# The first batch of a fused attention and MLP kernel: k cast by its transfer, masks added by TensorE, ranks for the first batch, and a first layer in two token ranges

## The chip, the cores and the metric

The kernel runs on one core of one Trainium2 chip. The metric is the device time in microseconds (us) of one execution, the lower the better; the median of several executions is quoted with its range. The figures of one profile are a little shorter than the time of its own execution, because the profile's span starts at the core's first instruction: the profiled execution of the kernel before took 351.13 us and has a span of 349.4.

Engine names: PE is TensorE (PEld its weight loads), DVE is VectorE, ACT is ScalarE, POOL is GpSimd, SP is SyncE.

## The reference, cut to what matters

```python
# q, k, v: (batch 8, heads 8, tokens 576, head size 64), float32
scores = 1/8 * q @ k^T
mask   = (0 <= i - j < 64)                    # causal, window of 64
attn   = softmax(where(mask, scores, -1e9))
x      = (attn @ v) -> (8 * 576 tokens, 512)
h      = x @ w_in                             # 512 x 2048
out    = (h * sigmoid(h)) @ w_out             # 2048 x 512, float32
```

## The kernel before

The program is written by a list scheduler, `Plan`. Every piece of work is added with a class, its cost on each engine that may do it, what it waits for, and a rank. `Plan.run()` plays the costs forward once, when the kernel is built, and always gives a free engine the ready piece with the lowest rank. What reaches the chip is a fixed order of instructions on each engine. So a rank or a cost in this table changes the order and nothing else; on the chip each engine waits for real.

```python
p = Plan(
    {name: len(b) for name, b in banks.items()},
    rank=dict(one=-9, dma=-1, ld0=-1, ld1=-1, st=-2, silu=-3, out=-2, pv=0, ot=0, s=1, moe=99, turn=2,
              norm=0, inverse=0, bridge=0, exp=1, mask=1, lift=2, shift=2, cast=4, late=5),
)
```

Attention is done in units of one head pair and 192 tokens, twelve to a batch. A batch starts by loading q and k, casting them to bf16 (`cast`), transposing them on PE (`turn`) and copying the result out of PSUM (`lift`); v is loaded with a cast and half of it is copied to the other 64 partitions (`shift`). A unit is then this chain:

```python
s  = p.add("s", {"PE": 0.17}, ...)                       # 3 matmuls: scores of keys against queries
ex = p.add("exp", {"ACT": 0.5}, ..., table="exp")
ma = p.add("mask", {"DVE": 0.37}, ..., [ex, c_mask[0]])  # exp times 0 or 1
pv = p.add("pv", {"PE": 0.17}, ...)                      # values, with a column of ones for the sum
rc = p.add("inverse", {"DVE": 0.21}, ...)
no = [p.add("norm", {"DVE": 0.37, "ACT": 0.8}, ...) for hh in range(2)]   # ACT only in batch 0
ot = p.add("ot", {"PE": 0.1}, ...)                       # matmul that transposes back
br = p.add("bridge", {"ACT": 0.34, "DVE": 0.36}, ...)    # to x, transposed, in SBUF
```

The MLP works on tiles of 512 tokens: 64 matmuls of the first layer, 16 silus on ACT, 64 matmuls of the second layer. The exponential and the silu are in different tables of ACT, and `Plan` reckons 1.28 us for each change (the trace has a table load of 1.28 us at 37.33). Tile 0 waits for the bridges of all twelve units of batch 0, since 512 tokens end in its third group:

```python
have = o_done[:NP * ((TB * (j + 1) + 2) // 3)]
...
op = p.add("moe", {"PE": 0.2165}, None, have + [win[ft // 2]], ...)
si = p.add("silu", {"ACT": 0.6}, ..., table="silu")
```

Batch 0's q comes through SP's queue, its k through ACT's, v and the weights through GpSimd's, cast to bf16 on the way. DVE clears the buffer of batch 1's transposed q (`clear_qk(1)`) at the start.

The softmax here doesn't subtract the row's maximum and nothing guards it: scores larger than these inputs give would overflow.

## Time and profile before

| what | figure | where from |
|---|---|---|
| time | 350.98 us (349.42 to 350.98, 3 runs) | timed runs |
| span of the profile | 349.4 us | the page |
| PE busy in the span | 321.9 us, 92% | the page, part 1 |
| first matmul of the MLP | 37.17 us | timeline |
| second layer of tile 0 starts | 60.10 us | timeline |
| first layer of tile 1 starts | 79.85 us | timeline |
| mean granted clock of PE | 0.995 | the run's record |

The prediction shows the stages. Two more views of the page matter later: the clock and the transfers in 40 equal slices of 8.7 us (in tenths), and the chain of work that ended last, by line.

```profile
PEclk9999999899999999999999999999999999999999
DMA  8999999696825967291963900010020011011011
...
PE mp L313 35%; PE mp L322 34%; PE at L284 5%; PE at L235 4%; PE at L270 4%; PE at L304 3%; DMA vv<-in_v_dram 2%; DVE ob L296 1%; DVE qbd L242 1%; ACT qbd L242 1%; ACT ob L300 1%; DVE e L279 1%; ACT g L319 1%; ACT e L276 1%; DVE qbd L184 1%
```

The clock row shows full almost throughout, though up to about 41 us the matmuls went at half pace all the same; the section on the result comes back to this. The transfers are near their fill for most of the first 60 us and busy on and off until about 200 us; after that they have room. The chain is PE's two MLP layers (L313 and L322, 69%) and PE's attention; everything else is a few per cent in all (DVE 6%, ACT 4%, transfers 2%), most of it at the start.

### The profile page before, as it was taken

Reading aid. Unit: us, or ns where it says so; the run is one execution under the profiler, and the core shown is the slowest. Engines: PE = TensorE matmul, PEld = TensorE weight load, DVE = VectorE, ACT = ScalarE, POOL = GpSimd, SP = SyncE. Lnnn points to the kernel's source line nnn. Section 1 sums busy time; section 2 is a strip of 40 time slices with the busy share of each in tenths; the row PEclk is TensorE's granted clock in tenths of the full one; section 3 lists DMA queues with packets and bytes.
Section 4 is the critical chain, followed back from the end, with each engine's and each line's share of the span. In section 5 each row is a group of like instructions: output and inputs, shape, how many; then the busy total and the mean of one; then the engine's idle time right before and its main releaser. Section 6 shows DMA issues by size and latency. Waiting matters only on the chain.

```text
span 349.4 us, 6381 instructions
## 1 busy us (share of the span) xinstructions
PE 321.9 (92%) x2356; PEld 177.5 (51%) x2400; DVE 198.2 (57%) x548; ACT 230.2 (66%) x450; POOL 52.3 (15%) x65
## 2 busy tenths in 40 slices
PE   1566897999999999999999999999999999999995
PEld 1444454655565555665556556655444444444442
DVE  7877395777958987888988896898200000000000
ACT  3667588438889888798968888766617525614611
POOL 8636650040000300211302200000000000000000
PEclk9999999899999999999999999999999999999999
DMA  8999999696825967291963900010020011011011
GB/s 213 188 214 288 188 236 251 57 59 183 243 76 168 188 199 218 70 106 49 137 202 74 85 2 30 34 60 2 0 92 30 0 62 60 0 63 60 0 56 66
DMA packets 61279, 37.64 MB, mean 108 GB/s; under 512 B 39232, under 2 KB 56128, under 8 KB 61248
## 3 DMA queue, kind: packets, MB, share of 16 engines
q0 software_dynamic: 44416, 11.28, 34.8%
q1 hardware_dynamic: 16000, 24.78, 22.7%
q10 hardware_dynamic: 832, 1.18, 1.3%
q8 instruction: 19, 0.31, 0.4%
q14 instruction: 12, 0.10, 0.1%
HBM read 36.70 MB, written 9.44 MB: 132 GB/s over the span
## 4 chain that ended last, share of the span: by engine, by line
PE 85%; DVE 6%; ACT 4%; DMA 2%; issue 2%; POOL 0%; ACTq 0%; DVEq 0%
PE mp L313 35%; PE mp L322 34%; PE at L284 5%; PE at L235 4%; PE at L270 4%; PE at L304 3%; DMA vv<-in_v_dram 2%; DVE ob L296 1%; DVE qbd L242 1%; ACT qbd L242 1%; ACT ob L300 1%; DVE e L279 1%; ACT g L319 1%; ACT e L276 1%; DVE qbd L184 1%
## 5 line engine op out<-in xcount | busy, mean ns | idle before, releaser
L322 PE MATMUL mp<-w_out_sb,g 128*128 128x512 bf16 x550 | 144.2, 381 | 0.9
L313 PE MATMUL mp<-bridge,w_in_sb 128*128 128x512 bf16 x558 | 134.9, 384 | 0.9 <-DMA vv<-in_v_dram 0.2
L319 ACT ACTIVATE g<-mp 128x512 bf16<-128x512 f32 x144 | 83.3, 597 | 22.6 <-PE mp L313 21.8
L313 PEld LDWEIGHTS <-w_in_sb 128*128 128x128 bf16 x576 | 53.5, 99 | 54.5 <-issue 3.0
L322 PEld LDWEIGHTS <-g 128*128 128x128 bf16 x576 | 52.8, 98 | 41.6 <-issue 0.3
L296 DVE TENSOR_TENSOR ob<-at,rc 64x192 bf16<-64x192 f32 x182 | 63.8, 351 | 4.8 <-ACT ob L300 1.3
L205 POOL DMA_DIRECT2D vv<-in_v_dram x32 | 33.0, 1034 | 128.3 <-PE at L284 109.1
L276 ACT ACTIVATE e<-at 128x384 bf16<-128x384 f32 x96 | 42.7, 497 | 9.2 <-PE at L270 8.7
L328 ACT COPY ot<-mp 128x512 f32<-128x512 f32 x23 | 13.4, 585 | 46.4 <-PE mp L322 45.0
L279 DVE TENSOR_TENSOR e<-e,mask 128x384 bf16<-128x384 bf16 x96 | 31.0, 349 | 18.3 <-ACT e L276 17.2
L284 PE MATMUL at<-vv,e 128*128 128x130 bf16 x288 | 32.7, 232 | 3.1 <-DVE ob L296 1.3
L270 PE MATMUL at<-qbd,kt 128*128 128x128 bf16 x288 | 29.6, 231 | 6.2 <-ACT qbd L242 2.6
L235 PE MATMUL at<-ident,natb 96*128 96x96 bf16 x384 | 27.0, 216 | 8.0 <-ACT natb L224 7.1
L284 PEld LDWEIGHTS <-e 128*128 128x128 bf16 x288 | 23.8, 102 | 18.6 <-DVE e L279 2.7
L309 ACT CAST bridge<-at 128x192 bf16<-128x192 f32 x62 | 19.6, 318 | 18.3 <-PE at L304 16.6
L235 PEld LDWEIGHTS <-natb 96*128 96x128 bf16 x384 | 22.6, 103 | 16.6 <-ACT natb L224 8.5
L270 PEld LDWEIGHTS <-kt 128*128 128x128 bf16 x288 | 22.2, 103 | 15.6 <-DVE kt L248 3.6
L304 PEld LDWEIGHTS <-ob 128*128 128x128 bf16 x288 | 19.6, 100 | 20.6 <-DVE ob L296 10.8
L304 PE MATMUL at<-twoi,ob 128*128 128x64 bf16 x288 | 25.5, 199 | 4.5 <-DVE ob L296 2.8
L242 DVE COPY qbd<-at 64x576 bf16<-64x576 bf16 x30 | 22.6, 752 | 9.8 <-PE at L235 8.1
L242 ACT COPY qbd<-at 64x576 bf16<-64x576 bf16 x34 | 21.5, 632 | 7.3 <-DVE qbd L242 6.4
L224 ACT CAST natb<-nat 96x768 bf16<-96x768 f32 x31 | 25.5, 828 | 0.8 <-DMA nat<-in_q_dram 0.8
(35 smaller groups left out, 144.0 us busy)
## 6 DMA issues: line engine op xcount, KB each, us to landing
out_dram<-ot SPq DMA_DIRECT2D x36, 256.0 KB, 2.0
nat<-in_q_dram SPq DMA_DIRECT2D x28, 288.0 KB, 4.5
nat<-in_k_dram SPq DMA_DIRECT2D x24, 288.0 KB, 4.9
vv<-in_v_dram POOLq DMA_DIRECT2D x32, 144.0 KB, 5.8
w_in_sb<-in_moe_w_in_dram POOLq DMA_DIRECT2D x8, 256.0 KB, 10.3
w_out_sb<-in_moe_w_out_dram POOLq DMA_DIRECT2D x8, 256.0 KB, 9.3
nat<-in_k_dram ACTq DMA_DIRECT2D x4, 288.0 KB, 7.2
nat<-in_q_dram POOLq DMA_DIRECT2D x4, 288.0 KB, 10.7
```

The lines of the kernel that those rows point to most:

```text
L205: queue[e].dma_start(out=vv[b % NK][:, 2 * g0 + 1:2 * g1 + 1:2, 0:D], in_=v[b].rearrange("h s d -> (h s) d").rearrange("(g p) d -> p g d", ...
L235: nc.tensor.matmul(pst[:, m], lhsT=natbs[w][:, m], rhs=ident[0:NR, 0:NR], is_transpose=True, start=(m == 0), stop=(m == NM - 1),)
L242: copies[e](out=qbd[b % NK][r, pj, hh].rearrange("x (p m) -> x p m", m=NM), in_=at_bf16(op)[r].rearrange("x (m p) -> x p m", m=NM),)
L270: nc.tensor.matmul(at_sp(op)[:, x], lhsT=kt[b % NK][:, pj * S + t * 64:pj * S + t * 64 + 128], rhs=qbd[b % NK][:, pj, :, t * 64:t * 64 + 6 ...
L276: nc.scalar.activation(out=es[n % NE], in_=at_sp(op), func=ACTF.Exp, scale=scale)
L279: nc.vector.tensor_mul(es[n % NE], es[n % NE], mask0 if g == 0 else mask)
L284: nc.tensor.matmul(at_pv(op)[:, x], lhsT=es[n % NE][:, x].rearrange("p h i -> p (h i)"), rhs=vv[b % NK][:, s:s + NB + 1:NB, 0:D + 1], star ...
L296: nc.vector.tensor_mul(ob[r, :, r], pv[r, :, hh, 0:D], rc[r, :, hh:hh + 1].to_broadcast([64, 3, 64]))
L304: nc.tensor.matmul(banks["at"][op["bank"]][:, 64 * x:64 * x + 64], lhsT=obs[n % NOB][:, x], rhs=twoi, start=(x == 0), stop=(x == 2))
L313: nc.tensor.matmul(banks["mp"][bank["bank"]], lhsT=w_in_sb[:, c, ft * 128:(ft + 1) * 128], rhs=bridge[c][:, j * TT:(j + 1) * TT], start=(c ...
L319: nc.scalar.activation(out=gts[gt], in_=banks["mp"][bank["bank"]], func=ACTF.Silu)
L322: nc.tensor.matmul(banks["mp"][bank["bank"]], lhsT=gts[gt][:, m * 128:(m + 1) * 128], rhs=w_out_sb[:, f, :], start=(f == 0), stop=(f == NF ...
```

## The change

Its intent is to start the MLP earlier. Batch 0 is the only batch that no matmul of the MLP hides, so every microsecond taken out of its chain should move the whole of the rest forward. Six things change for batch 0, for tile 0 and for the clearing. Besides, batch 2's q and k go to GpSimd's queue, `Plan` reckons transfers differently, and its rule for when scores may run among the MLP's matmuls is fitted to the two passes:

1. k is loaded by GpSimd with a cast, in two halves a head pair, straight into the bf16 buffer.
2. The mask is a bias of 0 or -30000, added to the scores by one more matmul; the multiplication on DVE goes.
3. Casts, lifts, shifts and exponentials rank above normalisations.
4. Units go group by group instead of pair by pair.
5. The clearing for batch 1 goes to GpSimd, behind w_in.
6. Tile 0's first layer is done for 384 tokens, which need eight units only, and then for the other 128.

```diff
+        rank0=dict(cast=-6, lift=-5, shift=-4.5, exp=-4, mask=-4, inverse=-3.5, norm=-3, bridge=-3.2),
...
+        for m, a in ((mask, bias), (mask0, bias0)):
+            nc.vector.tensor_scalar(a, m, 1.0, 30000.0, op0=ALU.subtract, op1=ALU.mult)
...
+    def load_k_cast(w, b, pj, hh):
+        nc.gpsimd.dma_start(
+            out=natbs[w][:, :, 64 * hh:64 * hh + 64],
+            in_=k[b, 2 * pj + hh].rearrange("(p m) d -> p m d", m=NM),
...
+    def scores_idle(op, b, pj, g):
+        nc.tensor.matmul(
+            banks["at"][op["bank"]][:, 0:384], lhsT=ident,
+            rhs=(bias0 if g == 0 else bias).rearrange("k x h i -> k (x h i)"), start=True, stop=False)
...  (the three score matmuls follow, with start=False)
-        for g, pj in ([(g, pj) for pj in range(NP) for g in range(NG)] if b == 0 else
-                      [(g, pj) for g in range(NG) for pj in range(NP)]):
+        for g, pj in [(g, pj) for g in range(NG) for pj in range(NP)]:
...
+        parts = [(0, 384), (384, TT)] if j == 0 else [(0, TT)]
+        for lo, hi in parts:
+            have = o_done[:NP * ((j * TT + hi + 191) // 192)]
...
-    c_qk.append(p.add("late", {"DVE": 1.8}, lambda _: clear_qk(1)))
+    c_q[1] = [p.add("dma", {"POOL": 1.3}, lambda e, hh=hh: clear_q(e, 1, hh)) for hh in range(2)]
...
-        lv = [p.add("dma", {"POOL": 1.0}, lambda e, part=part: load_v(e, b, part), busy, dma=2.6)
+        lv = [p.add("dma", {"POOL": 1.0}, lambda e, part=part: load_v(e, b, part), busy, dma=1.25)
```

## The prediction

> **What bounds the kernel now.** I cut the span into stages at places that the timeline names: the first matmul of the MLP (37.17), the end of its slow start (41.9), the end of tile 0's first layer (56.85), the start of its second layer (60.1) and of tile 1's first layer (79.85). The stage table gives each stage's start:end and length, then busy us (and instructions) of PE, PEld, DVE, ACT, POOL, then clock and DMA.
>
> ```profile
> 0.00:37.17 37.17, 18.05 (x156) 13.49 (x158) 28.66 (x84) 22.26 (x58) 23.83 (x36) 1.00 1.44 222
> 37.17:41.90 4.73, 4.73 (x16) 1.97 (x16) 0.00 (x0) 2.62 (x4) 3.41 (x6) 1.00 2.67 176
> 41.90:56.85 14.95, 14.84 (x114) 7.94 (x115) 12.56 (x22) 12.40 (x22) 5.07 (x5) 1.00 1.21 251
> 56.85:60.10 3.25, 1.29 (x12) 0.83 (x12) 1.39 (x6) 3.24 (x7) 0.00 (x0) 0.93 1.49 234
> 60.10:79.85 19.75, 19.56 (x157) 11.15 (x158) 14.70 (x49) 7.74 (x22) 4.00 (x4) 0.93 0.87 65
> 79.85:343.70 263.85, 261.56 (x1900) 141.48 (x1938) 140.92 (x389) 181.32 (x341) 15.98 (x16) 1.00 0.38 84
> ```
>
> From 60.1 on PE is 99% busy: that part is matmul work, which the change hardly touches. All that can be won lies before 60.1, where PE stands for 19.1 us before the MLP and for 2.0 us at 56.85. Before 37.17 the work is batch 0's attention, twelve units (four head pairs by three groups of 192 tokens), and it is paced by DVE (28.66 us busy) and ACT (22.26 us) handing work to each other. The timeline of the first us (start, duration, engine, line, what, and in brackets the idle time and its releaser) shows where that starts badly:
>
> ```profile
> 6.17 1.02 DVE L183 MEMSET qbd<- 64x1152 f32 x1 [0.18 <-issue]
> ...
> 7.47 1.02 DVE L184 MEMSET qbd<- 64x1152 f32 x1 [0.28 <-issue]
> 8.52 0.75 DVE L242 COPY qbd<-at 64x576 bf16<-64x576 bf16 x1
> ...
> 9.30 0.63 ACT L242 COPY qbd<-at 64x576 bf16<-64x576 bf16 x1 [2.67 <-DVE qbd L242]
> ```
>
> DVE clears batch 1's buffer while batch 0's first transposed q waits. At the other end the MLP starts:
>
> ```profile
> 36.32 0.64 PE L304 MATMUL at<-twoi,ob 128*128 128x64 bf16 x3 [0.44 <-ACT ob L300]
> ...
> 37.17 4.47 PE L313 MATMUL mp<-bridge,w_in_sb 128*128 128x512 bf16 x10 [0.22 <-DMA vv<-in_v_dram]
> 37.17 0.15 PEld L313 LDWEIGHTS <-w_in_sb 128*128 128x128 bf16 x1 [0.28 <-issue]
> 37.33 1.28 ACT L319 ACT_TABLE_LOAD   x1
> ```
>
> The chain of waits puts 7.90 us of a v transfer ahead of this matmul. I do not believe it: the matmul reads no v, and PE was idle for 0.22 us only. What it came after is the last unit's normalisation on ACT and its transpose on PE. So the start of the MLP is set by batch 0's last unit.
>
> **What the Trainium skill says.** (1) "TensorE: Matmul & The Clock Gate", "What's actually happening": a PE that has been idle runs at half clock until it has been busy for about 3.4 us. The trace agrees: the first weight loads of L313 come every 0.43 us, later 44 matmuls in a row take 9.66 us, 0.22 each. (2) "ScalarE: Activation LUTs", "What ACT_TABLE_LOAD costs": 1283 ns for the load, about 1380 more for a drain. The trace has 1.28 at 37.33; the silu after it starts at 38.70, so the drain does not show. (3) "DMA: Bandwidth & Descriptors", "SWDGE vs HWDGE vs iDMA": a cast in a transfer can only be issued from GpSimd. The change obeys it: k moves from ACT's queue to GpSimd's. (4) The same page, "Specifications": runs under 512 B do not reach full rate. The k cast writes runs of 64 bf16 elements, 128 B, as v does already; the four v transfers, issued from 1.5 to 4.5, land about 11.2 us later each, but among q, k and w_in, so no row here isolates that cost.
>
> **The change part by part**, with the order of instructions of the changed kernel at hand.
>
> *Clearing.* Batch 1's qbd goes to GpSimd behind w_in. DVE loses 2 x 1.02 plus gaps, 2.3 us, right on the path.
>
> *k by cast transfer.* Four casts of batch 0 vanish (0.83 on ACT or about 0.55 on DVE; the order shows two on each before), the fourth q's cast moves from DVE to ACT, and ACT no longer issues transfers until 3.0. GpSimd issues eight half transfers, then v, then w_in. The last pair's k reuses a buffer that waits for the first k's turn on PE, about 7 us, so v is issued some 7 us later (8.5 to 12.5 instead of 1.5 to 5.6). But v landed only at 12.7 to 15.5 before. With q and k mostly landed I expect 12.5 to 16, no loss. GpSimd keeps eight transfers outstanding (the fifth w_in issue, at 13.04, waited for the first v). So w_in still lands from about 17 to 28 (before: 16.5 to 27), q and k of batch 1 at 28 to 37, w_out at 43 to 54: the same stream, which already runs nearly full, DMA 9 tenths. It must stay ahead of an earlier MLP. Pass A (below) uses a w_in slice every 1.3 us from 27; w_out is wanted from about 51, one slice per 1.73 us. Both hold.
>
> *Masks as a bias.* Twelve multiplications of 0.35 leave DVE, 4.2 us, and a link of ACT to DVE to PE leaves each unit. Two bias tiles cost DVE some 0.6. PE gains twelve 384-column matmuls, 0.165 warm or 0.32 cold, 2 to 4 us in a stage where it was half idle.
>
> *Order.* Units run group by group instead of pair by pair, lifts first, and nine exponentials before most normalisations.
>
> *When the MLP can start.* It needs bridges of eight units. ACT's queue up to the eighth: four casts 3.3, four lifts 2.5, eleven exponentials 5.5, eight normalisations 8 x 0.71 = 5.7, three bridges 1.0: 18.0, from the first q at about 4.7: 22.7 with no waiting. DVE: free at 6.0, then eight lifts 6.0, masks 0.95, v shifts 8 x 0.32 = 2.6, ten reciprocals 2.0, ten normalisations 3.6, five bridges 1.6: 16.7, also 22.7. Two engines feeding each other do not run without gaps; DVE was 77% busy before. At 82 to 85% over the stage I get **27 instead of 37.17**, a gain of 10.2.
>
> *Tile 0 in two passes.* Pass A (384 tokens): 64 matmuls at 0.165, 10.5; six turn groups among them at 0.42, 2.5; a cold start about 1: 14, so 27 to 41. Then a new wait. ACT's queue holds, after the last silu (0.6): table load 1.28, three exponentials 1.5, a normalisation 0.71, another exponential 0.5, the last bridge 0.32: 4.9 until pass B may start, 45.9. PE has only some 2 us of scores and turns for that. Pass B is 64 x 0.055 = 3.5 of PE, but ACT goes first through a lift 0.63 and a table load 1.28, then sixteen silus of about 0.29 (estimate from 0.60 at 512 and 0.83 ns per element): about 5.5 for the stage. **The second layer starts at 51.4 instead of 60.1.** The split therefore returns some 1.5 of the 10.2: two more table loads and PE gaps of about 5.5 in all, against 2.0 before.
>
> *Sum.* 60.1 - 51.4 = 8.7. What follows is the same work for a busy PE. 351.0 - 8.7 = 342.3, rounded to **342**.
>
> **The rivals.** *(a) The transfers bound the start.* If the 128-byte runs make k and v slow in one queue, v lands after 18, values wait, the MLP starts at 30 or later: 345 to 348. For it: v now leaves after k, and DMA has no slack. Against it: bytes are the same, and 15.5 was the last v landing with everything competing. *(b) The two passes give the gain back.* If normalisations of the late units or batch 1's lifts queue ahead of the last bridge, the gap before pass B grows from 3 to 6 or more and PE turns cold again: 345 or more. For it: ACT runs in order and changes tables twice more. Against: batch 0's units are ranked first, and ACT was idle for part of 37 to 57. *(c) ACT and DVE run gapless and PE is warm when the MLP starts*, being denser: start at 25, no slow start: 339. *(d) Hidden anyway*: PE was never the bound before 37 and is after, so an earlier start cannot be swallowed unless w_out binds. It was complete at about 54 and in the new plan is not wanted whole before about 64.
>
> **Range and chances.** The start is uncertain by about 2.5 us each way, the gap and pass B by 2, the rest by 1: together about 3.5. Range 337.5 to 347. Faster by 2% means below 344.0, 2 us above my figure: 0.72. Within 2%: 0.27. Slower needs a stall of 16 us against the plan: 0.01.
>
> **What would show it.** Right: first L343 matmul at 25 to 29; no DVE clearing between 6 and the first lift; v shifts from about 13 without long waits; no mask multiplications before it; a PE gap of 2 to 4 us between passes with ACT's table load in it; second layer at 49 to 54; from there to the end 289.3, as before (349.4 - 60.1), within 1.5. Wrong: PE waiting for v, k or w_in (then a); a second layer that starts late although the first started early (then b); or a longer stretch after the second layer's start, if w_out or batch 1's attention now lags behind PE, which would mean that the gain of the start was only moved.

## More of the kernel before

Every timed run that is compared here was in the fast state. One run (`clear_first`) was a single look, whose state is unknown, and its time is not used.

## The result, and the profile after

The changed kernel took a median of 346.10 us (345.76 to 347.68), against 350.77 (349.42 to 350.98) of the kernel before in the same rounds: a ratio of 0.988, with a 95% interval of 0.985 to 0.992. A ratio here is the mean time of one kernel's fast runs over the mean of the other's fast runs of the same rounds, so it is not quite the ratio of the medians. The same kernel was timed twice more, in later sets (chips 12 and 3): 0.9944 (0.9908 to 0.998; 346.91 us) and 0.9906 (0.9875 to 0.9936; 346.03 us). So the gain is about 0.6 to 1.2%, two to four microseconds. The prediction had 2.5% and a range that ended at 347; the time fell inside the range and the gain is about a quarter to a half of what was forecast.

The first ratio may flatter the change a little. In the later sets every run of the kernel before at 350.1 us or more has a mean clock of 0.995, and every faster one has 1.000. Three of the four runs here have times of the slower group, and so has the profile shown above. The profile of the changed kernel is that of its slowest run (347.68; the others took 345.76 to 346.18).

The stage table of the changed kernel, cut at the same places and with one cut more for the second pass (columns as in the prediction: start:end, length, busy us and instructions of PE, PEld, DVE, ACT, POOL, clock, DMA share, GB/s):

```profile
0.00:30.99 30.99, 17.32 (x156) 12.61 (x157) 22.88 (x65) 17.87 (x47) 24.06 (x38) 0.90 1.30 158
30.99:45.38 14.39, 14.36 (x108) 8.68 (x106) 7.53 (x14) 11.22 (x22) 11.88 (x14) 0.86 1.78 216
45.38:50.81 5.43, 3.35 (x38) 2.31 (x36) 4.83 (x12) 4.42 (x10) 2.45 (x5) 0.81 1.21 227
50.81:57.82 7.01, 6.69 (x87) 6.58 (x86) 5.62 (x18) 5.80 (x19) 2.80 (x5) 0.66 1.13 262
57.82:77.81 19.99, 19.86 (x193) 12.00 (x191) 16.08 (x49) 17.17 (x33) 8.02 (x8) 1.00 1.86 205
77.81:346.00 268.19, 263.77 (x1906) 139.35 (x1905) 136.12 (x384) 171.95 (x329) 16.33 (x16) 1.00 0.37 82
```

The rows are: batch 0, pass A (384 tokens), the gap, pass B (128 tokens), the second layer of tile 0, and the rest. The MLP starts 6.2 us earlier than before (30.99 for 37.17). By the second layer 2.3 us of that is left (57.82 for 60.10). From there to the end it takes 288.2 us, 1.1 less than before (289.3), which with the 2.3 makes the 3.4 by which the span is shorter. The 1.1 need not be the change's: the profile before has 3.2 us at a clock of 0.50 there (59.8 to 63.0), and `before_clear`, without it, takes 288.3. DVE's and ACT's loads in the first row fell as reckoned (28.66 to 22.88, and 22.26 to 17.87), and POOL's is nearly the same.

The same two rows of slices, and the chain by line:

```profile
PEclk9995987999999999999999999999999999999999
DMA  9999999998796656979304800110020011011012
...
PE mp L352 36%; PE mp L343 35%; PE at L314 4%; PE at L253 4%; PE at L288 4%; PE at L334 3%; DMA natb<-in_k_dram 2%; DVE qbd L260 2%; ACT qbd L260 1%; ACT ob L330 1%; DVE vv L274 1%; DVE ob L326 1%; DVE kt L266 1%; DVE vv L276 1%; PE at L300
```

Two things are new in these views. In three slices between 26 and 61 us PE's clock is 0.5 to 0.8, where the row before showed full. That row has to be checked against the pace of the matmuls. In the kernel before, the first ten matmuls of the MLP took 4.47 us (shown in the prediction; their weight loads are 0.43 us apart), twice the 0.22 of later ones, and three score matmuls in a row took 0.52 us at 29.20 against 0.33 at 58.67: half pace, at a shown clock of 1.00. In the changed kernel the pace changes from half (0.53 at 17.37) to full (0.33 at 18.00), again at a shown 1.00. So in these profiles the row tells nothing before its first recorded change, both kernels start at half pace, and both enter the MLP at half pace. And the transfer on the chain is no longer v but `natb<-in_k_dram`, the cast transfer of k. The timeline shows the start of that:

```profile
9.06 1.12 PE L253 MATMUL at<-ident,natb 96*128 96x96 bf16 x12 [3.70 <-DMA natb<-in_k_dram]
...
30.99 1.47 PE L343 MATMUL mp<-bridge,w_in_sb 128*128 128x384 bf16 x4
```

PE turns the first q at 4.70, then waits 3.70 us for the first k. Its two half transfers, issued at 1.56 and 2.3, took 6.9 and 6.7 us to land; the plain transfer of the first k before took 4.5 us from 0.7. And the gap between the passes, as ACT sees it (start, us, engine, line, what, count):

```profile
45.93 1.28 ACT L306 ACT_TABLE_LOAD   x1
47.22 1.25 ACT L306 ACTIVATE e<-at 128x384 bf16<-128x384 f32 x3
48.62 0.71 ACT L330 ACTIVATE ob<-at,rc 64x64 bf16<-64x64 f32 x3
49.23 0.47 ACT L306 ACTIVATE e<-at 128x384 bf16<-128x384 f32 x1
50.16 0.32 ACT L339 CAST bridge<-at 128x192 bf16<-128x192 f32 x1 [0.46 <-PE at L334]
50.93 0.63 ACT L260 COPY qbd<-at 64x576 bf16<-64x576 bf16 x1 [0.45 <-DVE qbd L260]
51.58 1.28 ACT L349 ACT_TABLE_LOAD   x1
```

This is the list that the prediction gave, in the same order: back to the exponential's table, three exponentials, a normalisation, one more exponential, the last bridge; then a lift and the silu's table. The gap is 5.4 us for a predicted 4.9.

### The profile page after: what moved, and what is told of

Same layout as the page of the kernel before. It is cut to its first block, busy times and chain, and to the rows that moved or that the text cites. A ratio compares the mean times of both kernels' runs of the same rounds, so it can differ in the third digit from the quotient of the medians.

```text
span 346.0 us, 6606 instructions
## 1 busy us (share of the span) xinstructions
PE 325.4 (94%) x2476; PEld 181.5 (52%) x2476; DVE 193.1 (56%) x539; ACT 228.4 (66%) x457; POOL 65.5 (19%) x83
## 4 chain that ended last, share of the span: by engine, by line
PE 87%; DVE 6%; ACT 3%; DMA 2%; issue 1%; POOL 0%; DVEq 0%; POOLq 0%; ACTq 0%
PE mp L352 36%; PE mp L343 35%; PE at L314 4%; PE at L253 4%; PE at L288 4%; PE at L334 3%; DMA natb<-in_k_dram 2%; DVE qbd L260 2%; ACT qbd L260 1%; ACT ob L330 1%; DVE vv L274 1%; DVE ob L326 1%; DVE kt L266 1%; DVE vv L276 1%; PE at L300 1%
## 5 line engine op out<-in xcount | busy, mean ns | idle before, releaser
L352 PE MATMUL mp<-w_out_sb,g 128*128 128x512 bf16 x576 | 148.4, 379 | 0.0
L343 PE MATMUL mp<-bridge,w_in_sb 128*128 128x512 bf16 (+2 forms) x640 | 140.7, 367 | 0.5 <-ACT g L349 0.3
L349 ACT ACTIVATE g<-mp 128x512 bf16<-128x512 f32 (+2 forms) x160 | 86.0, 554 | 23.6 <-PE mp L343 21.6
L343 PEld LDWEIGHTS <-w_in_sb 128*128 128x128 bf16 x640 | 59.2, 102 | 51.3 <-issue 1.9
L358 ACT COPY ot<-mp 128x512 f32<-128x512 f32 x29 | 16.9, 586 | 53.8 <-PE mp L352 49.2
L309 DVE TENSOR_TENSOR e<-e,mask 128x384 bf16<-128x384 bf16 x84 | 27.0, 347 | 6.8 <-ACT e L306 6.0
L288 PE MATMUL at<-qbd,kt 128*128 128x128 bf16 x252 | 25.5, 219 | 0.9 <-DVE kt L266 0.5
L320 DVE RECIPROCAL rc<-at 128x6 f32<-128x6 f32 x96 | 18.2, 193 | 12.5 <-PE at L314 10.2
L260 DVE COPY qbd<-at 64x576 bf16<-64x576 bf16 x27 | 20.2, 748 | 8.5 <-ACT qbd L260 6.3
L288 PEld LDWEIGHTS <-kt 128*128 128x128 bf16 x252 | 18.3, 97 | 9.1 <-issue 1.1
```

The lines of the kernel that those rows point to most:

```text
L260: copies[e](out=qbd[b % NK][r, pj, hh].rearrange("x (p m) -> x p m", m=NM), in_=at_bf16(op)[r].rearrange("x (m p) -> x p m", m=NM),)
L288: nc.tensor.matmul(at_sp(op)[:, x], lhsT=kt[b % NK][:, pj * S + t * 64:pj * S + t * 64 + 128], rhs=qbd[b % NK][:, pj, :, t * 64:t * 64 + 6 ...
L309: nc.vector.tensor_mul(es[n % NE], es[n % NE], mask0 if g == 0 else mask)
L343: nc.tensor.matmul(banks["mp"][bank["bank"]][:, lo:hi], lhsT=w_in_sb[:, c, ft * 128:(ft + 1) * 128], rhs=bridge[c][:, j * TT + lo:j * TT + ...
L349: nc.scalar.activation(out=gts[gt][:, lo:hi], in_=banks["mp"][bank["bank"]][:, lo:hi], func=ACTF.Silu)
L352: nc.tensor.matmul(banks["mp"][bank["bank"]], lhsT=gts[gt][:, m * 128:(m + 1) * 128], rhs=w_out_sb[:, f, :], start=(f == 0), stop=(f == NF ...
```

## The experiments

All of them change the changed kernel, unless a text says otherwise. This table has the places of each profile in us and the time; the sets were timed on three chips (sets 1, 2 and 4 on chip 12, set 3 on 14, set 5 on 3), each beside the kernel before, so ratios compare across sets and medians only within one. "Second" is the start of tile 0's second layer, "tile 1" that of tile 1's first layer.

| kernel | MLP | second | tile 1 | median (range) | ratio (95%) |
|---|---|---|---|---|---|
| changed, first profile | 30.99 | 57.82 | 77.81 | 346.10 (345.76 to 347.68) | 0.988 (0.985, 0.992) |
| set 1: k_first_plain | 27.47 | 55.64 | 75.51 | 348.12 (347.08 to 349.64) | 0.996 (0.992, 1.001) |
| k_all_plain | 30.20 | 56.01 | 75.75 | 346.25 (345.12 to 346.87) | 0.990 (0.986, 0.994) |
| clear_dve | 29.03 | 56.16 | 75.54 | 346.38 (345.79 to 346.99) | 0.992 (0.987, 0.996) |
| one_pass | 34.94 | 53.23 | 74.62 | 345.84 (345.36 to 346.66) | 0.990 (0.986, 0.994) |
| set 2: after_again | 30.45 | 57.08 | 77.07 | 346.91 (346.02 to 349.62) | 0.994 (0.991, 0.998) |
| warm | 30.52 | 55.48 | 75.41 | 345.51 (345.27 to 345.93) | 0.990 (0.986, 0.994) |
| mask_mul | 30.91 | 59.75 | 79.82 | 349.89 (349.20 to 350.97) | 1.003 (0.999, 1.006) |
| no_ranks | 31.46 | 58.32 | 78.31 | 348.67 (348.19 to 349.60) | 0.999 (0.996, 1.003) |
| set 3: exp_first | 31.40 | 50.09 | 70.05 | 346.04 (344.26 to 348.18) | 0.988 (0.982, 0.994) |
| exp_first_warm | 32.80 | 51.06 | 70.96 | 348.16 (344.59 to 349.35) | 0.992 (0.986, 0.998) |
| one_pass_warm | 34.90 | 53.40 | 74.73 | 345.59 (344.13 to 345.92) | 0.985 (0.981, 0.990) |
| before_clear | 37.30 | 58.08 | 77.01 | 348.72 (348.17 to 350.61) | 0.996 (0.992, 1.000) |
| set 4: exp_first_lessv | 32.37 | 52.27 | 72.22 | 343.28 (342.35 to 343.51) | 0.981 (0.976, 0.986) |
| after_lessv | 29.85 | 56.73 | 76.73 | 346.60 (345.56 to 346.65) | 0.991 (0.986, 0.995) |
| exp_first_v26 | 32.33 | 55.57 | 75.46 | 345.52 (345.30 to 346.09) | 0.988 (0.984, 0.992) |
| set 5: best | 32.70 | 54.72 | 75.15 | 345.28 (342.56 to 345.64) | 0.986 (0.983, 0.990) |
| after_third | 30.17 | 55.56 | 75.55 | 346.03 (345.24 to 347.11) | 0.991 (0.988, 0.994) |

The theory was that the first k lands late and holds up batch 0's whole chain. Its rivals were that DVE is slowed by what GpSimd does beside it, that PE's half clock costs the time, and that the early start is real but is taken back later by something that the kernel then runs into.

### k back to the plain transfer: the first one, or all

```diff
-                if b == 0 and kk:
+                if b == 0 and kk and not (pj == 0):       # k_first_plain; k_all_plain: never
...
+                    (else) cls, us = ("ld1", {"ACT": 0.45})   # k through ACT's queue, then a cast
```

> The changed kernel, but the first pair's k of batch 0 is loaded as before (ACT's queue, then a cast); the other three pairs keep the cast in the transfer. Theory K (the first k lands at 9.0 instead of about 5.3, PE stands 3.7 us for it, and that delay carries through to the MLP): first k lands near 5.3, first scores near 8 instead of 10.5, first matmul of the MLP near 28.5 instead of 31.0, total 2 us less than the changed kernel (344). Rival P (DVE and GpSimd stand in each other's way at 15 to 24 us, v shifts 0.7 to 1.1 us instead of 0.32, and that backlog sets the start whatever k does): start of the MLP moves by less than 1 us, total within 1 us.

> The changed kernel with all four k of batch 0 loaded and cast as before: only the cast transfer undone. v and w_in are then issued some 7 us earlier. Theory K: first k near 5.3, MLP starts near 28.5 or a little later because four casts (0.55 to 0.83 us) return to DVE and ACT; total 1 to 2.5 us less than the changed kernel. Rival P: the casts return 2 to 3 us of work to the two engines that set the start, so the MLP starts at 31 to 33 and the total is 0 to 2 us more.

With the first k alone by the plain transfer, PE turns it at 7.04, where the three profiles of the changed kernel have 9.06, 8.51 and 8.24:

```profile
7.04 1.14 PE L253 MATMUL at<-ident,natb 96*128 96x96 bf16 x12 [0.45 <-DVE natb L242]
...
27.47 1.16 PE L343 MATMUL mp<-bridge,w_in_sb 128*128 128x384 bf16 x3
```

The MLP starts at 27.47, where the prediction had put it. In the three profiles of the changed kernel the start follows the first k at a fixed distance: 30.99 - 9.06 = 21.93, 30.45 - 8.51 = 21.94, 30.17 - 8.24 = 21.93 (and in `after_lessv`, below, 29.85 - 7.91 = 21.94). So the late k does delay the start. Here the distance is shorter too, 20.43. DVE's eight copies of v were all over before GpSimd's clearing began and took 3.3 us, where the changed kernel's first profile has 4.9; the next experiment is about that. The miss of 4.0 us is thus made of k's landing, 1.2 to 2.0 us, and of a longer way from there.

But the time did not improve: 348.12, with a ratio that is no better than the changed kernel's in any of its three sets. Pass A took 14.9 us, the gap 6.4, pass B 6.8, and from tile 1 to the end it took 269.8 us, against 268.2 in the changed kernel. An earlier start of the MLP is not an earlier end.

With all four k's by plain transfers the first k is turned at 7.07 as well, but the start is 30.2: four casts are back on ACT and DVE, and the distance is 23.1. The time is the changed kernel's. So the cast transfer of k gives with one hand what it takes with the other, and nothing measurable in time comes of it.

### Clearing by DVE instead of GpSimd

```diff
-    c_q[1] = [p.add("dma", {"POOL": 1.3}, lambda e, hh=hh: clear_q(e, 1, hh)) for hh in range(2)]
+    c_q[1] = [p.add("clear", {"DVE": 1.05}, lambda e, hh=hh: clear_q(e, 1, hh)) for hh in range(2)]
```

> The changed kernel with batch 1's qbd cleared by DVE when it is free, not by GpSimd behind w_in. Theory P: the v shift that took 1.11 us while GpSimd cleared (21.45 to 23.65) falls to 0.7 or below, MLP starts 0.5 to 1 us earlier, total 0 to 1 us less. Theory K: start unchanged within 0.5 us, total the same.

> clear_dve once more, one look, beside the runs above on one chip: the MLP's start at 29.0 in its first profile against 30.5 to 31.0 in two profiles of the changed kernel. If GpSimd's clearing costs the start 1.5 us, it comes again at 28.5 to 29.5; if it was chance, 30 to 31.

(`clear_first` is the same file again, for a second profile.) The ground for it was in the changed kernel's timeline. First DVE's copies of v to the other partitions, then what GpSimd did at that time:

```profile
18.64 0.71 DVE L274 COPY vv<-vv 64x576 bf16<-64x576 bf16 x1
...
22.22 0.47 DVE L276 COPY vv<-vv 64x576 bf16<-64x576 bf16 x1
22.72 1.11 DVE L274 COPY vv<-vv 64x576 bf16<-64x576 bf16 x1
```

```profile
15.41 6.00 POOL L229 DMA_DIRECT2D w_in_sb<-in_moe_w_in_dram  x8
21.45 2.20 POOL L194 MEMSET qbd<- 64x1152 f32 x2
```

The same copy, which takes 0.32 us at its shortest, takes up to 0.71 us beside the issues and up to 1.11 beside the memsets. The eight together took 4.9 us where the prediction had 8 x 0.32 = 2.6. With the clearing on DVE, later, the last two copies read:

```profile
20.87 0.32 DVE L276 COPY vv<-vv 64x576 bf16<-64x576 bf16 x1
21.22 0.41 DVE L274 COPY vv<-vv 64x576 bf16<-64x576 bf16 x1
```

and in `clear_first` 0.32 and 0.32. The MLP's start came 20.72 and 20.63 us after the first k instead of 21.93, so 1.2 us earlier; 0.7 of that are the copies (4.2 us in all), and the rest came with the order, which changes a little. This fits the lock that the Trainium skill describes in "SBUF — State Buffer", section "Who interferes with whom": a copy on DVE can take the port pair that it shares with GpSimd, and whichever is second blocks fully. The trace agrees for the memsets. Whether the issues do the same is open: here most copies beside the w_in issues remain at 0.71, but in `k_first_plain` all eight lay beside them (13.76 to 19.89) and took 0.31 to 0.65. In time the experiment is a tie (346.38).

### Tile 0's first layer in one pass

```diff
-        parts = [(0, 384), (384, TT)] if j == 0 else [(0, TT)]
+        parts = [(0, TT)]
```

> The changed kernel with tile 0's first layer in one pass of 512 tokens. Theory S (the split gives back what the early start wins: two more table loads, a 5.4 us gap and a half-clock stretch at 48 to 55): MLP starts near 34, first layer ends near 51, second layer starts near 54.5 instead of 57.8, total 1.5 to 3 us less than the changed kernel. Rival (the split is worth its cost, since PE does 10 us of first layer while the last units finish): second layer starts at 58.5 or later, total 1 us or more above the changed kernel.

The MLP starts 4 us later (34.94), needs no second pass, and reaches the second layer at 53.23, 2.3 to 4.6 us before the three profiles of the changed kernel. Its time, 345.84, is at least as good. So the split buys an early start and pays it back in full: the gap and pass B are 12.4 us in the changed kernel, and 0.5 us here. From the second layer to the end it takes 290.6 us, 2.4 more than in the changed kernel's first profile, so a part of its own lead is lost later too.

### The changed kernel again, with a warm clock, and with one part undone

```diff
+    # warm: 40 idle matmuls of 256 columns while PE waits for the MLP, 16 more between the passes
+    for cls, n, gate, deps in (("warm1", 40, no_mlp_yet, [g_pv[0]]), ("warm2", 16, a_done, [])):
...
-                if b:                                     # mask_mul: batch 0 multiplies by its mask again
+                if True:
-                s["fn"] = lambda _, s=s, pj=pj, g=g: (scores if b else scores_idle)(s, b, pj, g)
+                s["fn"] = lambda _, s=s, pj=pj, g=g: scores(s, b, pj, g)
...
-        rank0=dict(cast=-6, lift=-5, shift=-4.5, exp=-4, ...)        # no_ranks
+        rank0=dict(),
```

> The changed kernel once more, unaltered, for the spread of its start and its clock. If the late start of the MLP (31.0) belongs to the kernel, it comes again within 0.5 us. If part of it was the half clock that lay over 24.4 to 34.7 in the first profile (theory H: PE works at half clock in other stretches in each run), start and total go with the mean clock: a run at clock 0.985 has the MLP near 29 to 30 and is 1.5 us shorter than one at 0.975.

> The changed kernel with 40 matmuls of no use (256 columns, into banks that the MLP does not use yet) between batch 0's last scores and the MLP, and 16 between the two passes, so that PE does not fall to half clock. Results are untouched. Theory H: no half clock between 20 and 60, pass A loses under 1 us (2.3 before), the stage from pass B to the second layer under 1.2 us (2.5 before), total 2 to 3 us less than the changed kernel. Rival (waiting for ACT and DVE alone makes these stages long): clock near full but stages as long, total within 1 us.

> The changed kernel with batch 0's masks multiplied by DVE again, no bias matmuls. If the bias is worth what I put down (12 multiplications of 0.35 off DVE and a link less per unit): MLP starts 2.5 to 4 us later, total 1 to 3 us more. If PE's 12 extra matmuls of 384 columns (2 us at full clock, 4 at half) cost as much as they save: start within 1 us, total within 1 us or less by up to 2, which is the PE work saved.

> The changed kernel without the special ranks of batch 0 (lifts, casts and exponentials no longer ahead of normalisations). Theory: ranks and group order make the early start. Then the MLP starts 2 to 4 us later and the total is 1.5 to 3 us more. Rival: order does not matter once DVE and ACT are busy; start within 1 us.

The clock first. Stretches of 10 us, of `after_again` and then of `warm` (columns as in the stage table; the clock is the third figure from the right):

```profile
20.00:30.00 10.00, 5.87 (x49) 3.94 (x48) 7.88 (x28) 6.47 (x28) 7.41 (x11) 0.70 1.41 210
50.00:60.00 10.00, 9.62 (x108) 8.26 (x108) 6.86 (x21) 8.72 (x24) 5.53 (x7) 0.76 1.11 267
```

```profile
20.00:30.00 10.00, 7.84 (x91) 6.11 (x89) 7.53 (x27) 6.33 (x27) 7.33 (x10) 1.00 1.40 217
50.00:60.00 10.00, 8.58 (x103) 6.39 (x105) 6.71 (x22) 8.05 (x24) 6.01 (x8) 1.00 1.11 282
```

The idle matmuls keep the clock at 1.00. The MLP starts at the same time (30.52 for 30.45), so the half clock after 20 us does not explain the late start. The half pace before 18 us is a rival that no run tested, since the idle matmuls begin at 20.06. In the chain of the changed kernel that ended last, PE's own pieces between 9.06 and 17.27 add up to 4.9 us at half pace; at full pace about 2.4 of it would go (an estimate, half of the sum). Pass A then takes 12.8 us instead of 14.2, and the second layer starts 1.6 us earlier. By the medians the time is 1.4 us shorter (345.51 for 346.91); the intervals of the ratios overlap. In this profile the half clock therefore costs the changed kernel about 1.5 us. The change did not bring it in: the kernel before starts its first layer at half pace too, ten matmuls at 0.43 us instead of 0.22, about 2.1 us. It also varies: in `after_third` it lasted 3.4 us around the second pass instead of 6.8, and the second layer started at 55.56 without any help.

The parts next. Without the bias (`mask_mul`) the MLP starts just as early, at 30.91, and yet the kernel is as slow as the kernel before: 349.89, ratio 1.003. Here the order came out worse. ACT loads a table at 47.79, 49.59, 51.40, 53.58 and 59.74, alternating between an exponential or two and a silu or a few; the gap grows to 6.2 us and the second layer starts at 59.75. Without the ranks (`no_ranks`) the start is 1.0 us later and the time 1.8 us longer. The loss without the bias is clear of the noise (0.999 to 1.006, against 0.991 to 0.998 with it); the loss without the ranks is likely, but its interval of 0.996 to 1.003 overlaps. The bias's share shows up after the start, in what the order does with ACT, not in the chain of batch 0 where the prediction had put it. That is what this one order shows: the bias was not taken out with the order held fixed.

### All exponentials of batch 0 before the MLP starts

Tile 0's first layer is made to wait for the twelve exponentials, so that no table change is left between the passes. Three kernels: this alone, with 44 idle matmuls, and the one-pass kernel with the same 44.

```diff
-            have = o_done[:NP * ((j * TT + hi + 191) // 192)]
+            have = o_done[:NP * ((j * TT + hi + 191) // 192)] + (exps[:NP * NG] if j == 0 else [])
```

> The changed kernel, with one dependency more: tile 0's first matmul waits until the exponentials of all twelve units of batch 0 are done, so the twelfth unit comes before ACT changes to the silu table and pass B needs no way back to the exponential table. Theory G (the 12.4 us from the end of pass A to the second layer are mainly that way back: two table loads, three foreign exponentials, the last unit's chain): MLP starts up to 1 us later, pass B follows pass A within 0.5 us, the second layer starts near 51 to 52.5 instead of 57, and the total falls by 2 to 4 us. Rival W (what is not done before the second layer, batch 1's attention, is only put behind it): second layer starts as early, but the stage from it to the end grows by as much as is won, total within 1 us.

> The same with 44 matmuls of no use before the MLP, so that PE starts it at full clock. Theory H (half clock over the start of pass A): no half clock between 20 and 45, pass A 1 to 1.5 us shorter, total 1 to 1.5 us less than without them. Rival: within 0.5 us.

> Tile 0 in one pass of 512 tokens, with 44 matmuls of no use before the MLP. Against one_pass: half clock (13.7 us from 23.6 in its profile) gone, first layer about 1.2 us shorter, total 1 to 1.5 us less. Against exp_first_warm: if the split itself is worth something once the way back to the exponentials is gone, one_pass_warm is 1 us or more slower; if not, they are within 0.7 us.

It did what it was made for. The gap shrank to 0.6 us, pass B to 1.4, and the second layer started at 50.09: 5.5 to 7.7 us earlier than in the three profiles of the changed kernel, and earlier than the 51.4 of the prediction. Tile 1 started at 70.05. And the time did not move: 346.04, with two runs near 344.4 and two near 347.9. The profile is of one of the slower two (347.56). In it the second layer to the end took 295.7 us instead of 288.2. Two stretches and three lines of the timeline of `exp_first` show where:

```profile
80.00:85.00 5.00, 2.94 (x18) 1.32 (x17) 0.45 (x1) 3.37 (x6) 0.00 (x0) 1.00 1.15 257
85.00:90.00 5.00, 2.24 (x16) 1.42 (x17) 3.92 (x6) 0.63 (x1) 0.00 (x0) 0.73 0.27 87
```

```profile
50.09 2.11 PE L352 MATMUL mp<-w_out_sb,g 128*128 128x512 bf16 x8
...
85.59 0.75 DVE L276 COPY vv<-vv 64x2304 bf16<-64x2304 bf16 x1 [5.15 <-DMA vv<-in_v_dram]
...
87.76 0.66 PE L253 MATMUL at<-ident,natb 96*128 96x96 bf16 x6 [4.76 <-DVE natb L242]
```

At 83.0 PE stops for 4.76 us: it wants a transposition whose input DVE has not cast. DVE had been standing for 5.15 us in front of a copy of v, and that v, issued at 68.07, landed at 85.5, 17.4 us later. Until about then the transfers are busy throughout. The kernel had come to work that its data had not reached. With idle matmuls the stall is still there (`exp_first_warm`: 4.32 us before 88.23, ratio 0.992). Neither kernel's faster runs (344.3 to 344.6) were profiled, so how long they stall is not known.

The one-pass kernel with a warm clock had a ratio of 0.985 (0.981 to 0.990), the lowest of the right kernels; it is just apart from the changed kernel's 0.994 (0.991 to 0.998), but not from its other two.

### The clearing alone, on the kernel before

> The kernel before with one part of the change alone: batch 1's buffers cleared by GpSimd behind w_in, not by DVE at the start. If the start of the first lift carries through, as I reckoned: first lift near 6.3 instead of 8.5, MLP 2 us earlier (35), total 2 us less than before. If batch 0 is paced later by something else (k, v, or DVE and ACT): MLP within 0.7 us, total within 1 us.

```diff
-    c_qk.append(p.add("late", {"DVE": 1.8}, lambda _: clear_qk(1)))
+    c_qk.append(p.add("dma", {"POOL": 2.6}, lambda _: clear_qk(1, nc.gpsimd)))     # behind w_in
```

DVE's clearing leaves the start and the first lift goes earlier (6.46 for 8.52), but the MLP starts at 37.30, as before. The 2.3 us that the prediction called "right on the path" were not on it. The later places in the table (58.08 and 77.01, against 60.10 and 79.85) are not to be compared: this profile is of a run with a clock of 1.000, the one of the kernel before of a run with 0.995. The ratio of 0.996 (0.992 to 1.000) does not settle whether anything came of it.

### Fewer bytes of v, and another order

To tell a transfer limit from an order that happens to be bad, two kernels load only one ninth of v for batches 2 and 3. Their results are wrong on purpose; everything else is the same. A third kernel tells the scheduler that a v transfer costs 2.6 us, as the kernel before did, so that it plans around the wait.

```diff
-        g0, g1 = part * 9, part * 9 + 9
+        g0, g1 = part * 9, part * 9 + (1 if b in (2, 3) else 9)                      # ..._lessv
...
-        lv = [p.add("dma", {"POOL": 1.0}, lambda e, part=part: load_v(e, b, part), busy, dma=1.25)
+        lv = [p.add("dma", {"POOL": 1.0}, lambda e, part=part: load_v(e, b, part), busy, dma=2.6 if b else 1.25)   # exp_first_v26
```

> exp_first, but the v transfers of batches 2 and 3 bring one ninth of their rows (wrong result on purpose; every engine's order stays the same). Theory T (the stream of transfers is the bound once PE runs ahead): the stall at 83 to 88 is gone, what was won by 70 us is kept, total 3.5 to 5.5 us less than exp_first (about 341). Rival: the stall stays, total within 1 us.

> The changed kernel with the same thinner v transfers in batches 2 and 3. If the transfers do not bind in the changed kernel as it is (it has no PE wait over 0.5 us after 58): total within 0.7 us of it. If they already hold it back: 1.5 us or more less.

> exp_first with the planner told that a v transfer from batch 1 on takes 2.6 us of the stream, as in the kernel before, not 1.25; nothing else. Only the order changes: DVE's v copies come later against its casts. Theory O (the order on DVE makes the stall): no PE wait above 1 us between 70 and 95, total 3 us or more less than exp_first. Theory T (the stream is full anyway): waits of 3 us or more in all remain somewhere between 60 and 100, total within 1.5 us of exp_first.

With less v the stall of `exp_first` is gone. In `exp_first_lessv` PE is busy through the first of the same two stretches (and for 4.90 us of the second), and DVE works instead of waiting:

```profile
80.00:85.00 5.00, 4.94 (x31) 2.41 (x31) 4.87 (x9) 4.59 (x9) 0.00 (x0) 1.00 0.67 206
```

From the second layer to the end it took 289.5 us, like the kernel before, and the ratio fell to 0.981 (0.976 to 0.986, which just touches the 0.982 to 0.994 of `exp_first` in its own set). The changed kernel itself gains nothing from less v (346.60, ratio 0.991). So v's transfers stall a kernel whose second layer starts 10 us before that of the kernel before (50.09 for 60.10), and do not hold back one that is 2.3 to 4.5 us ahead. `exp_first_v26` has no such stall, but the second layer is back at 55.57: the early second layer was given up for it. Its time of 345.52 is like the others'.

### The best combination

This is `exp_first_v26` with 44 idle matmuls ahead of the MLP, beside the changed kernel in the same rounds.

> exp_first_v26 (345.5) with 44 matmuls of no use between batch 0's last scores and the MLP. Theory H: the 13.7 us at half clock from 22.0 (3.4 us of it inside pass A, which begins at 32.3) goes, clock above 0.99, total 1 to 2 us less: 343.5 to 344.5, and 2 to 3 us less than the changed kernel in the same rounds. Rival: pass A waits for ACT and the transfers anyway, total within 0.7 us of 345.5.

> The changed kernel for the third time. Expected from two sets of rounds (0.988 and 0.9944 of the kernel before): 346.0 to 347.0, clock 0.975 to 0.985, ratio 0.988 to 0.994; MLP start 21.9 us after the first k's transposition begins, as in both earlier profiles (9.06 to 30.99, 8.51 to 30.45).

The results are right, the mean is 344.7 us against 346.1, and the ratios are 0.986 (0.983 to 0.990) and 0.991 (0.988 to 0.994). The intervals overlap: whether it beats the changed kernel is not settled. It does beat the kernel before.

## Why the prediction was wrong

The direction was right and the time lay at the upper end of the range, but the gain was forecast at 8.7 us and is 3.4 in the span. In the first profile the second layer starts at 57.8 instead of 51.4. The 6.4 us between them divide by the prediction's own terms like this (in `after_third`, a faster run, 4.2 are missing: start 30.2, pass A 13.2, gap 5.7, pass B 6.5):

| step of the prediction | forecast | measured | short by |
|---|---|---|---|
| start of the MLP | 27 | 31.0 | 4.0 |
| pass A | 14 | 14.4 | 0.4 |
| gap between the passes | 4.9 | 5.4 | 0.5 |
| pass B and silus | 5.5 | 7.0 | 1.5 |
| second layer to the end | 289.3 | 288.2 | -1.1 |

**The start: the term that failed.** "At 82 to 85% over the stage I get 27 instead of 37.17, a gain of 10.2." The gain was 6.2. The work of ACT and DVE was counted "from the first q at about 4.7". But a score needs k too, and k's landing was nowhere in the sum: k's cast transfer was said to come with "no loss" to v, and its own landing was not asked for. The first k was turned at 9.06, after a wait of 3.70 us, and `k_first_plain` shows a start at 27.47 with a first k that is earlier by 1.2 to 2.0 us and shifts that are shorter by 1.6. A second part is those shifts, 4.9 us instead of 2.6: moving GpSimd's clearing away from them brought the start about 1.2 us closer to the first k (`clear_dve`, `clear_first`). A third part may be PE, which the sum left out: from 9.0 to 18.0 it was busy for 8.45 of 9.00 us, at half pace, and no run shows what that costs the start. The same part of the sum counted the removal of DVE's own clearing as "right on the path"; `before_clear` shows no earlier start from it.

**The passes: mechanism right, pass B too short.** The gap is the predicted list of ACT's work, within half a microsecond. Pass A and pass B ran partly at half clock (0.86 and 0.66). The prediction allowed "a cold start about 1" for pass A and nothing for pass B. `warm` gives 1.6 us back in all, but even with a full clock pass B took 6.6 us, so the rest of its excess is not explained by the clock. The prediction said that the split returns "some 1.5 of the 10.2". From the MLP's start to the second layer it takes 26.8 us instead of 22.9, so 3.9 of the 6.2 went there, and `one_pass` shows that without the split nothing is lost in time.

**The sum: a step that the changed kernel did not test, and that fails once the lead is larger.** "What follows is the same work for a busy PE." In the changed kernel it held: 288.2 us, within the 1.5 that was allowed. But `exp_first` brought the second layer to 50.1, ahead of the forecast, and the total stayed at 346.0. The lead was lost at 83 to 88 us in a wait for v, and `exp_first_lessv`, where the stall is gone, shows that it was v's bytes. So 342 would probably not have come out even with the start at 27 and the passes as forecast; no run had exactly that. The prediction checked that w_in and w_out stay ahead of an earlier MLP; it did not check q, k and v of batches 2 and 3, which an earlier PE also wants earlier.

**The rivals.** (a) "The transfers bound the start" named the right place and mostly the wrong transfer: it was k, and v did not land late enough to be waited for long. Its figure, 345 to 348, is what came. (b) "The two passes give the gain back" holds in part, as said above. (c) is refuted: the starts were 30.2 to 31.0, and the MLP began at half pace. (d) "Hidden anyway" was dismissed because "an earlier start cannot be swallowed unless w_out binds". It was swallowed, by v, when the second layer started 10 us early (`exp_first`).

**What else the prediction said would show:** no clearing by DVE before the first lift, v shifts from about 13 (first at 15.47, in step with the later k), no mask multiplications in batch 0, the table load in the gap: all seen. The time with the mask multiplication back says that the gain goes with the bias, but that the bias acts through the order after the start and not through the 4.2 us that it takes off DVE before it.

**What stays open:** what PE's half pace before 18 us costs the start; why pass A of `exp_first` takes 16.7 us; why `k_first_plain` needs 1.6 us more from tile 1 to the end and so loses what it won; why copies of v beside w_in's issues took 0.7 us in one order and half of that in another; and what part of a lead of 5 to 10 us the transfers let through. Each order that the scheduler makes differs in many places at once, so a difference of a microsecond between two of them is not always one cause's.

## What to carry to other kernels

When a chain of work at the start is to be shortened, list every input of its first step with the time at which it lands, and start the count at the last of them, not the first. When a stage is moved forward, go on down the timeline and ask of each later transfer whether it can be earlier too: here v, in a stream of transfers that was more than nine tenths busy, did not come earlier with the engines. And when a fixed order is rebuilt by a scheduler, undo the parts one by one, since the part that pays (here the mask as a bias) may pay somewhere other than where it took work away.

## What the Trainium skill lacked or had wrong

- "DMA: Bandwidth & Descriptors", "Anatomy of one DMA — SWDGE (gpsimd) path", gives about 2.0 us plus bytes over 436 GB/s for a transfer issued by GpSimd. For the 72 KB that a half k writes that is about 2.2 us (an estimate from the page's fit); the runs show 6.9 and 6.7 us to landing at the start of the kernel, with q's transfers beside it, and 4.5 us for the plain 288 KB transfer on ACT's queue. A figure for casts in 128-byte runs beside other queues is missing.
- "SBUF — State Buffer", "Who interferes with whom", has the lock between DVE and GpSimd and factors (a DVE 6.8 times slower), but no durations for a copy beside a memset. Here one bf16 copy of 64x576 on DVE took 0.32 us at its shortest, 0.31 to 0.71 beside GpSimd's transfer issues, and up to 1.11 beside its memsets, 3.5 times as long. The page's box on transfers issued by GpSimd warns of DVE holding GpSimd up; here, beside the memsets, DVE was the one held up.
- "TensorE: Matmul & The Clock Gate", "What's actually happening", says of the ramp's cost that it is under 1% of a typical span, and that one shouldn't fit a count of slow matmuls. In `warm` it was worth about 1.5 us, 0.4%, which agrees, but it is as large as the differences that were to be told apart: stretches of half clock of 3.4 to 13.7 us came and went between kernels and between runs of one kernel. The kernel before itself falls into two groups: in the last set its runs at a mean clock of 1.0 average 348.8 us and those at 0.995 average 350.7, a difference of about half of what the change was worth or more.
- "ScalarE: Activation LUTs", "What ACT_TABLE_LOAD costs", adds about 1380 ns of drain to the load. In every gap looked at, the next activation starts right behind the load: 45.93 plus 1.28 is 47.21, and the exponentials start at 47.22.
